# Attention, gated feed-forward and expert layer on one core: sweeps of 2, 3, 2 and 5 hidden units in place of 3, 2, 2 and 5, another order of weight conversions, one normalising product per head pair

## The chip, the core and the metric

The kernel runs on one core of one Trainium2 chip. The metric is the device time of one execution in microseconds (us). Before the change three runs gave 655.58, 655.60 and 659.03 us, median 655.6 us. One further execution was profiled; its own time was 655.69 us.

## What is computed

Three layers follow each other on 2 x 768 = 1536 tokens of 512 features.

```python
# 1. attention, 8 heads of 64: 8 global keys and the last 96 local ones, a slope per head
a = softmax(q @ k.T / 8 - slope * dist, kept keys only);  x = a @ v
# 2. gated layer, 512 -> 1536 -> 512
xn = x / sqrt(mean(x * x) + 1e-6) * rms_g
x = (silu(xn @ w_gate) * (xn @ w_val)) @ w_out
# 3. of 8 experts (512 -> 1024 -> 512) each token takes the one with the largest logit
out = p_max * (relu(x @ w1[e]) @ w2[e])
```

The weights of layer 2 (w_gate, w_val, w_out) come as 64-bit floats. Layers 2 and 3 multiply in a split form: each operand is a high part and the rest, and three products (high x high, high x rest, rest x high) make one.

## The kernel before, in words

Tokens are worked on in six stages of two tiles (256 tokens). The 1536 hidden features of layer 2 are 12 units of 128 (`m` = 0 to 11).

**Attention** (`fast_attention`, L410) takes 24 pairs of heads, four for each stage, and two tiles of each: 48 steps. A step computes scores on TensorE (L533 to L550), adds the distance table and takes the extremum on VectorE (L557), exponentiates on ScalarE (L561), transposes on TensorE (L572), copies the result on ScalarE (L580) and multiplies by the values (L601). After both tiles of a pair, `values` normalises: L608 and L609 make the reciprocals, and L611 multiplies, once for each tile. The first eight pairs use q and k as they are; from the ninth on they are split (L486 and L498 on ScalarE, L489 on GpSimd, L499 on VectorE). When the four pairs of a stage are done, `tail` (L381) normalises its rows and transposes them (L400, L403, L404); the stage is then "ready" for layer 2.

**Layer 2** (`moe_block`, L757) does a few units for one stage. A unit is 24 matmuls of 256 columns (L769: 12 with the gate weights, 12 with the value weights), then L777 to L787 on ScalarE, VectorE and GpSimd; after the units of a block, two tiles of output are accumulated, three matmuls of 512 columns for each unit and tile (L806). Sweep 0 writes the output sum to the tile (L813, ScalarE); later sweeps add to it (L815, VectorE). Sweep 0 goes over units 0 to 2 for all stages, the second sweep over 3 and 4, the third over 5 and 6, and the last over 7 to 11 (`M0`, `M1`, `range(lo, hi)`).

**Weight conversions** (`prep_steps`, L361): each unit needs three, gate, value and out. `load64` (L320) issues a 512 KB load on SyncE's queue into one of three `raw` buffers. `convert64` (L328) turns the 64-bit words into a high part and a rest: L334 on ScalarE, L337, L340, L343 and L346 on VectorE into one of two `cv` buffers, L353 on ScalarE, and L354 for the rest, on GpSimd during attention and on VectorE afterwards (`pin["sweep"]`). The results lie in a pool `wp` with three slots and a pool `ea` with four; `ea` shares its memory with attention's buffers and opens when attention has ended.

**Order.** The loop at L1165 writes the program: after each attention step it takes from `PREPS` which conversions are due (L1175), and for each step a credit of 0.5 (`MOE_RATE`) for matmuls of sweep 0 on stages that are ready. What is left of sweep 0 comes after attention (L1211) with one conversion of the next group (`PM[1]`) at each yield; the second and third sweep carry `PM[2]` and `PM[3]`, one conversion at every fourth or fifth yield (L1214). This is the order of priority; a scheduler with a model of time then sets the fixed order of each engine's instructions, and takes one that was written later where it finds an engine free and the operands and buffers there. A conversion written during attention is held behind the exponential of its step (L335); one of `PM[1]` has no such bond.

Of the kernel before, what the change touches and what calls it, by code (L numbers as in the profile page):

```python
# [14 lines left out]
ALU = mybir.AluOpType  # L15
# [4 lines left out]
P = 128  # L20
# [25 lines left out]
def kernel(  # L46
# [22 lines left out]
    FIRST = [0, 1, 1, 1, 1]  # L69
    M0 = [3] * NSTAGE  # L70
    M1 = 7
    PM = [[0, 1, 2], [3, 4, 5, 6], [7, 8, 9], [10, 11]]
    NHID = 6
# [3 lines left out]
    NRAW = 3  # L77
    PREPS = [2, 4, 6, 7, 11, 12, 20, 28, 36]
    NA = 3
# [210 lines left out]
    def body(is_fast):  # L290
# [69 lines left out]

        def prep_steps(ms, pool, nslot):  # L361

            steps = []
            for m in ms:
                def gv(i, w, m=m):
                    if i == 0:
                        weights[m, 0] = pool.tile([P, 2, 2, KD, P], F32R, tag="gv", bufs=nslot, name=f"gv{m}")
                    t = weights[m, 0]
                    raw = load64(w[:, m * P:(m + 1) * P].bitcast(U32).rearrange("(k p) f -> p k f", p=P), KD)
                    convert64(raw, t[:, i, 0].rearrange("p k f -> p (k f)"), t[:, i, 1].rearrange("p k f -> p (k f)"))  # L370

                def ow(m=m):
                    t = weights[m, 1] = pool.tile([P, 2, DM], F32R, tag="ow", bufs=nslot, name=f"ow{m}")
                    raw = load64(w_out[m * P:(m + 1) * P, :].bitcast(U32).rearrange("p (a f) -> p a f", a=1), 1)
                    convert64(raw, t[:, 0], t[:, 1])

                steps += [lambda gv=gv: gv(0, w_gate), lambda gv=gv: gv(1, w_val), ow]
            return steps

# [30 lines left out]
        def fast_attention(pool):  # L410
# [174 lines left out]
            def values(g, t, ptf, nb):  # L585
# [19 lines left out]
                if t == nt - 1:  # L605
                    rc = pool.tile([P, ST, 2], F32, tag="rc", bufs=2, name="rc")
                    xs3 = xp[:, 0:nt * VW].rearrange("p (t c) -> p t c", c=VW)
                    nc.vector.tensor_scalar(out=rc[:, 0:nt], in0=xs3[:, :, 0:VW:VW - 1], scalar1=1e-9, scalar2=None, op0=ALU.add)  # L608
                    nc.vector.reciprocal(rc[:, 0:nt], rc[:, 0:nt])  # L609
                    for tt in range(nt):  # L610
                        nc.vector.tensor_tensor(  # L611
                            out=part[STARTS[st] + tt][:, hp * P:(hp + 1) * P].rearrange("p (j d) -> p j d", j=2),
                            in0=xp[:, tt * VW + 1:tt * VW + 1 + P].rearrange("p (j d) -> p j d", j=2),
                            in1=rc[:, tt].unsqueeze(2).to_broadcast([P, 2, D]), op=ALU.mult,
                        )
                    groups[g] = None
# [537 lines left out]
        att = fast_attention(apool) if is_fast else dense_attention(apool)  # L1154
        preps = prep_steps(PM[0], wp, 3)
        ready = []
# [8 lines left out]
        while True:  # L1165
# [7 lines left out]
            if is_fast and nun == LATE:  # L1173
                late_loads()
            while preps and nun > PREPS[9 - len(preps)]:  # L1175
                preps.pop(0)()
            credit += MOE_RATE
            while True:
                if moe is None and ready:
                    st = ready.pop(0)  # L1180
                    moe = moe_block(0, range(M0[st]), st, mpool, False)
                    credit = 0.0
# [12 lines left out]
        ea = ea_cm.__enter__()  # L1195
        nx = prep_steps(PM[1], ea, 4)

# [13 lines left out]
        for st in ready:  # L1211
            run(moe_block(0, range(M0[st]), st, mpool, False))
        drain(f() for f in nx)
        for lo, hi, ms, pool, nslot, every in ((3, 5, PM[2], wp, 3, 4), (5, M1, PM[3], ea, 4, 5)):  # L1214
            nx = prep_steps(ms, pool, nslot)
            for st in range(NSTAGE):
# [163 lines left out]
```

## Time and profile before

| | before |
|---|---|
| median of three runs | 655.6 us |
| the profiled execution: its time / its span | 655.69 us / 654.0 us |
| granted TensorE clock, mean | 0.988 |
| TensorE matmul busy, weight load busy | 628.9 us (96%), 562.3 us (86%) |
| VectorE, ScalarE, GpSimd busy | 446.2, 320.3, 208.7 us (68%, 49%, 32%) |
| L769: 1728 matmuls; L806: 432 | 228.2 us; 113.9 us |

The span runs from the first to the last instruction of the profiled execution; 1.7 us of its time lie outside. Engines are PE (TensorE matmul), PEld (its weight load), DVE (VectorE), ACT (ScalarE), POOL (GpSimd) and SP (SyncE). Matmuls are pipelined, so busy times of neighbours overlap. Times in rows are counted from the start of the span.

### The profile page before, as it was taken

How to read it: one execution, taken by the hardware profiler on the slowest of the kernel's cores; microseconds unless marked ns; L12 is line 12 of the kernel's file. 1: busy time of each engine (PE TensorE's matmuls, PEld its weight loads, DVE VectorE, ACT ScalarE, POOL GpSimd, SP SyncE). 2: the span in 40 equal slices, each digit the busy share in tenths (PEclk: the TensorE clock that was granted, in tenths of full speed). 3: DMA queues.
4: the chain of work that ended last, by engine and by line, in shares of the span. 5: the costliest groups of instructions: out<-in, count | busy, mean ns of one | idle time of the engine just before them, and what ended most of it. 6: DMA issues, size and time to landing. Idle time of an engine off the chain costs nothing. (4 is left out here: it accounts for less than half of the span.)

```text
span 654.0 us, 11691 instructions
## 1 busy us (share of the span) xinstructions
PE 628.9 (96%) x4280; PEld 562.3 (86%) x4281; DVE 446.2 (68%) x1098; ACT 320.3 (49%) x624; POOL 208.7 (32%) x275
## 2 busy tenths in 40 slices
PE   9998998899999999999999999999999999999992
PEld 4667887899999999999999999997888899899891
DVE  5765888976599988676359998944667464664410
ACT  3666798777555533334622221333656564654420
POOL 4415758663122212111222532461610221011010
PEclk9999899899999999999999999999999999999997
DMA  7536466551044532131311010442978667454000
GB/s 228 158 90 201 127 174 181 157 149 39 1 130 130 161 98 72 59 98 65 129 65 65 2 65 34 122 138 82 301 261 261 206 217 253 168 189 140 17 13 30
DMA packets 56567, 82.98 MB, mean 127 GB/s; under 512 B 7983, under 2 KB 38703, under 8 KB 56496
## 3 DMA queue, kind: packets, MB, share of 16 engines
q1 hardware_dynamic: 53552, 74.75, 36.9%
q0 software_dynamic: 2944, 7.35, 3.4%
q8 instruction: 37, 0.61, 0.4%
q14 instruction: 34, 0.28, 0.1%
HBM read 75.75 MB, written 7.39 MB: 127 GB/s over the span
## 5 line engine op out<-in xcount | busy, mean ns | idle before, releaser
L769 PE MATMUL pg<-xn,gv 128*128 128x256 f32 x1728 | 228.2, 285 | 1.2 <-DVE th L778 1.2
L769 PEld LDWEIGHTS pg<-xn,gv 128*128 128x128 f32 x1728 | 220.2, 192 | 8.2 <-DVE th L778 1.5
L787 POOL TENSOR_TENSOR hid<-hf,hid 128x256 fp32r<-128x256 f32 x72 | 61.4, 855 | 174.6 <-ACT hid L786 174.5
L806 PE MATMUL po<-ow,hid 128*128 128x512 f32 x432 | 113.9, 394 | 0.0
L1017 PE MATMUL py<-ew,eh 128*128 128x512 f32 x384 | 91.2, 395 | 0.9 <-DVE eh L1084 0.5
L1017 PEld LDWEIGHTS py<-ew,eh 128*128 128x128 f32 x384 | 71.3, 188 | 17.7 <-DVE eh L1084 0.9
L806 PEld LDWEIGHTS po<-ow,hid 128*128 128x128 f32 x432 | 75.5, 189 | 11.7 <-POOL hid L787 0.3
L1039 PE MATMUL ph<-xs,ew 128*128 128x256 f32 x672 | 83.1, 283 | 0.0
L1039 PEld LDWEIGHTS ph<-xs,ew 128*128 128x128 f32 x672 | 81.6, 191 | 0.7
L786 ACT ACTIVATE hid<-hf 128x256 fp32r<-128x256 f32 x72 | 29.9, 417 | 83.7 <-DVE hf L782 81.9
L1024 POOL DMA_INDIRECT out_dram<-yo,tk x16 | 16.5, 1034 | 139.1 <-ACT yo L1023 107.7
L838 DVE CUSTOM_DVE_ANT_0 jk<-duo,rgb 128x512 bf16<-128x512 f32 x64 | 54.3, 849 | 0.5
L561 ACT ACTIVATE pr<-pr,mx 128x256 f32<-128x256 f32 (+1 forms) x96 | 45.1, 484 | 14.0 <-DVE mx L557 13.2
L957 DVE TENSOR_TENSOR ew<-rawe,ew 128x1024 fp32r<-128x1024 f32 (+1 forms) x36 | 40.8, 1134 | 12.9 <-ACT ew L953 12.9
L1048 DVE SCALAR_TENSOR_TENSOR eh<-ph,eh 128x256 fp32r<-128x256 f32 x56 | 23.1, 423 | 37.5 <-ACT eh L1047 35.5
L777 ACT ACTIVATE th<-pg 128x256 f32<-128x256 f32 x72 | 27.2, 379 | 39.8 <-PE pg L769 37.3
L957 DVE TENSOR_TENSOR ew<-duo,ew 128x1024 fp32r<-128x1024 f32 x28 | 34.1, 1224 | 17.9 <-ACT ew L953 16.8
L953 ACT ACTIVATE ew<-rawe 128x1024 fp32r<-128x1024 f32 x36 | 38.0, 1059 | 10.2 <-PE pg L769 4.6
L778 DVE SCALAR_TENSOR_TENSOR th<-th,pg 128x256 f32<-128x256 f32 x72 | 29.7, 415 | 16.4 <-ACT th L777 15.4
L1047 ACT ACTIVATE eh<-ph 128x256 fp32r<-128x256 f32 x56 | 21.2, 384 | 39.2 <-PE ph L1039 38.1
L953 ACT ACTIVATE ew<-duo 128x1024 fp32r<-128x1024 f32 x28 | 29.4, 1059 | 19.4 <-PE py L1017 19.4
L815 DVE TENSOR_TENSOR duo<-duo,po 128x512 f32<-128x512 f32 x36 | 23.4, 684 | 18.7 <-PE po L806 18.6
(178 smaller groups left out, 935.8 us busy)
## 6 DMA issues: line engine op xcount, KB each, us to landing
rawe<-in_moe_w_dram SPq DMA_DIRECT2D x36, 512.0 KB, 5.0
duo<-in_moe_w_dram SPq DMA_DIRECT2D x28, 512.0 KB, 5.4
raw<-in_moe_w_gate_dram SPq DMA_DIRECT2D x12, 512.0 KB, 3.8
raw<-in_moe_w_val_dram SPq DMA_DIRECT2D x12, 512.0 KB, 5.6
raw<-in_moe_w_out_dram SPq DMA_DIRECT2D x12, 512.0 KB, 3.4
kn<-in_k_dram SPq DMA_DIRECT2D x28, 192.0 KB, 3.3
qn<-in_q_dram SPq DMA_DIRECT2D x36, 128.0 KB, 2.9
vn<-in_v_dram SPq DMA_DIRECT2D x16, 192.0 KB, 2.6
```

Of the source, the lines that this page charges most:

```text
L561: pin["act"] = nc.scalar.activation(out=pr[:, j, 0:n], in_=pr[:, j, 0:n], func=ACTF.Exp, bias=mx[:, t, j:j + 1], scale=-1.0,)
L769: nc.tensor.matmul(out=pg[:, 0:n_], lhsT=gv[:, i, a, kk, :], rhs=x[st][:, kk, :], start=(n == 0), stop=(n == 3 * KD - 1),)
L777: pin["th"] = nc.scalar.activation(out=th, in_=pss[0][:, 0:n_], func=ACTF.Tanh, scale=0.5)
L778: nc.vector.scalar_tensor_tensor(out=th, in0=th, scalar=1.0, in1=pss[0][:, 0:n_], op0=ALU.add, op1=ALU.mult)
L786: nc.scalar.activation(out=hh[:, 0], in_=hf, func=ACTF.Copy)
L787: nc.gpsimd.tensor_tensor(out=hh[:, 1], in0=hf, in1=hh[:, 0].bitcast(F32), op=ALU.subtract)
L806: nc.tensor.matmul(out=po, lhsT=hid[mi][:, a, t * P:(t + 1) * P], rhs=ow[:, c, :], start=(mi == 0 and n == 0), stop=(mi == len(ms) - 1 and ...
L838: nc.vector.tensor_tensor_reduce(out=jk, in0=part[i0 + t], in1=rgb[e // 4][:, e % 4, :], scale=1.0, scalar=0.0, op0=ALU.mult, op1=ALU.add, ...
L953: cp = nc.scalar.activation(out=t[:, 0], in_=raw, func=ACTF.Copy)
L957: nc.vector.tensor_tensor(out=t[:, 1, 0:nd], in0=raw[:, 0:nd], in1=t[:, 0, 0:nd].bitcast(F32), op=ALU.subtract)
L1017: last_mm["py"] = nc.tensor.matmul(out=py, lhsT=hid(m, a, j), rhs=w2t[m // 2][:, c, (m % 2) * DM:(m % 2 + 1) * DM], start=(n == 0), stop=( ...
L1039: nc.tensor.matmul(out=ph[:, 0:CAP], lhsT=w1t[kk][:, a, m * P:(m + 1) * P], rhs=x[:, kk, :], start=(n == 0), stop=(n == 3 * KD - 1),)
```

## The change

Sweep 0 takes two units, the second sweep three (2, 3, 4). The groups of conversions are `[0, 1]`, `[2, 3, 4]`, `[5, 6, 7, 8]` and `[9, 10, 11]`, in place of `[0, 1, 2]`, `[3, 4, 5, 6]`, `[7, 8, 9]` and `[10, 11]`. During attention six conversions are due, after steps 2, 4, 6, 8, 11 and 18, and gate and value of both units come ahead of the two out weights. `slot` gives each unit the pool that it had. The third sweep takes a conversion at every fourth yield in place of every fifth. L611 becomes one product for both tiles of a pair.

```diff
--- before.py
+++ after.py
@@ -67,15 +67,15 @@
     XT = "ccccss"
     RING = "ccceewweec"
     FIRST = [0, 1, 1, 1, 1]
-    M0 = [3] * NSTAGE
+    M0 = 2
     M1 = 7
-    PM = [[0, 1, 2], [3, 4, 5, 6], [7, 8, 9], [10, 11]]
+    PM = [[0, 1], [2, 3, 4], [5, 6, 7, 8], [9, 10, 11]]
     NHID = 6
     MOE_RATE = 0.5
     NDV = 512
     HP = 0
     NRAW = 3
-    PREPS = [2, 4, 6, 7, 11, 12, 20, 28, 36]
+    PREPS = [2, 4, 6, 8, 11, 18]
     NA = 3
     MMA = "mm mm mm s s"
     MMB = "mm mm mm s s"
@@ -358,11 +358,15 @@
         weights = {}
         pin = {"act": None, "dve": None, "th": None, "sweep": False}
 
-        def prep_steps(ms, pool, nslot):
-
-            steps = []
+        def slot(m):
+            return (wp, 3) if m in (0, 1, 2, 7, 8, 9) else (ea, 4)
+
+        def prep_steps(ms, ow_last=False):
+
+            steps, ows = [], []
             for m in ms:
                 def gv(i, w, m=m):
+                    pool, nslot = slot(m)
                     if i == 0:
                         weights[m, 0] = pool.tile([P, 2, 2, KD, P], F32R, tag="gv", bufs=nslot, name=f"gv{m}")
                     t = weights[m, 0]
@@ -370,12 +374,14 @@
                     convert64(raw, t[:, i, 0].rearrange("p k f -> p (k f)"), t[:, i, 1].rearrange("p k f -> p (k f)"))
 
                 def ow(m=m):
+                    pool, nslot = slot(m)
                     t = weights[m, 1] = pool.tile([P, 2, DM], F32R, tag="ow", bufs=nslot, name=f"ow{m}")
                     raw = load64(w_out[m * P:(m + 1) * P, :].bitcast(U32).rearrange("p (a f) -> p a f", a=1), 1)
                     convert64(raw, t[:, 0], t[:, 1])
 
-                steps += [lambda gv=gv: gv(0, w_gate), lambda gv=gv: gv(1, w_val), ow]
-            return steps
+                steps += [lambda gv=gv: gv(0, w_gate), lambda gv=gv: gv(1, w_val)]
+                (ows if ow_last else steps).append(ow)
+            return steps + ows
 
 
         def tail(st, pool):
@@ -607,12 +613,11 @@
                     xs3 = xp[:, 0:nt * VW].rearrange("p (t c) -> p t c", c=VW)
                     nc.vector.tensor_scalar(out=rc[:, 0:nt], in0=xs3[:, :, 0:VW:VW - 1], scalar1=1e-9, scalar2=None, op0=ALU.add)
                     nc.vector.reciprocal(rc[:, 0:nt], rc[:, 0:nt])
-                    for tt in range(nt):
-                        nc.vector.tensor_tensor(
-                            out=part[STARTS[st] + tt][:, hp * P:(hp + 1) * P].rearrange("p (j d) -> p j d", j=2),
-                            in0=xp[:, tt * VW + 1:tt * VW + 1 + P].rearrange("p (j d) -> p j d", j=2),
-                            in1=rc[:, tt].unsqueeze(2).to_broadcast([P, 2, D]), op=ALU.mult,
-                        )
+                    nc.vector.tensor_tensor(
+                        out=duo[st][:, :, hp * P:(hp + 1) * P].rearrange("p t (j d) -> p t j d", j=2),
+                        in0=xs3[:, :, 1:P + 1].rearrange("p t (j d) -> p t j d", j=2),
+                        in1=rc[:, 0:nt].unsqueeze(3).to_broadcast([P, nt, 2, D]), op=ALU.mult,
+                    )
                     groups[g] = None
 
             warm(WARM1)
@@ -1152,7 +1157,8 @@
         apool_cm = tc.tile_pool(name="attn", bufs=1, side="right")
         apool = apool_cm.__enter__()
         att = fast_attention(apool) if is_fast else dense_attention(apool)
-        preps = prep_steps(PM[0], wp, 3)
+        preps = prep_steps(PM[0], True)
+        npreps = len(preps)
         ready = []
         moe = None
         credit = 0.0
@@ -1172,13 +1178,13 @@
             nun += 1
             if is_fast and nun == LATE:
                 late_loads()
-            while preps and nun > PREPS[9 - len(preps)]:
+            while preps and nun > PREPS[npreps - len(preps)]:
                 preps.pop(0)()
             credit += MOE_RATE
             while True:
                 if moe is None and ready:
                     st = ready.pop(0)
-                    moe = moe_block(0, range(M0[st]), st, mpool, False)
+                    moe = moe_block(0, range(M0), st, mpool, False)
                     credit = 0.0
                 if moe is None or credit <= 0:
                     break
@@ -1193,7 +1199,7 @@
         pin["act"], pin["sweep"] = None, True
         ea_cm = tc.tile_pool(name="ea", bufs=1, side="right")
         ea = ea_cm.__enter__()
-        nx = prep_steps(PM[1], ea, 4)
+        nx = prep_steps(PM[1])
 
         yields = [0]
 
@@ -1209,10 +1215,10 @@
         if moe is not None:
             run(moe)
         for st in ready:
-            run(moe_block(0, range(M0[st]), st, mpool, False))
+            run(moe_block(0, range(M0), st, mpool, False))
         drain(f() for f in nx)
-        for lo, hi, ms, pool, nslot, every in ((3, 5, PM[2], wp, 3, 4), (5, M1, PM[3], ea, 4, 5)):
-            nx = prep_steps(ms, pool, nslot)
+        for lo, hi, ms, every in ((M0, 5, PM[2], 4), (5, M1, PM[3], 4)):
+            nx = prep_steps(ms)
             for st in range(NSTAGE):
                 run(moe_block(1, range(lo, hi), st, mpool, False), every)
             drain(f() for f in nx)
```

## Rows read from the trace of the kernel before

**Rows 1.** Windows: us, then PE, PEld, DVE, ACT, POOL busy, granted clock, DMA share, GB/s

```profile
50.00:65.00 15.00, 12.77 (x100) 10.63 (x99) 7.25 (x30) 9.09 (x18) 8.42 (x10) 1.00 0.67 192
65.00:82.00 17.00, 15.78 (x117) 14.78 (x117) 15.30 (x38) 13.72 (x30) 12.57 (x21) 0.90 0.47 127
82.00:98.00 16.00, 15.03 (x123) 13.97 (x123) 13.98 (x55) 14.81 (x36) 8.73 (x13) 1.00 0.61 175
98.00:115.00 17.00, 14.99 (x113) 13.72 (x112) 14.68 (x46) 14.14 (x32) 13.85 (x20) 1.00 0.68 175
115.00:131.00 16.00, 13.80 (x99) 13.09 (x98) 15.05 (x35) 11.91 (x26) 11.13 (x14) 0.89 0.58 161
131.00:147.00 16.00, 16.00 (x133) 15.61 (x132) 11.50 (x44) 11.81 (x26) 10.66 (x19) 1.00 0.55 153
```

**Rows 2.** Waits of TensorE, 0 to 180 us: us in total, times, longest

```profile
PE sp L550 <- DVE mx L557: 4.6, 7, 1.4
PE pp L572 <- ACT ptS L580: 2.2, 1, 2.2
PE pg L769 <- DVE th L778: 1.2, 1, 1.2
```

**Rows 3.** Windows of L769 alone: us, PE and PEld busy (x instructions), clock, DMA

```profile
82.00:98.00 16.00, 2.13 (x12) 1.62 (x12) 1.00 0.61 175
98.00:115.00 17.00, 3.77 (x24) 3.11 (x24) 1.00 0.68 175
```

**Rows 4.** Timeline of TensorE, first block's output: start, us, engine, line

```profile
102.17 2.89 PE L806 MATMUL po<-ow,hid 128*128 128x512 f32 x12
...
126.06 1.08 PE L806 MATMUL po<-ow,hid 128*128 128x512 f32 x4
```

**Rows 5.** Timeline of ScalarE: conversions begin (L334), stages become ready (L403)

```profile
64.27 0.58 ACT L403 ACTIVATE xn<-trx 128x512 fp32r<-128x512 f32 x1
...
77.49 0.66 ACT L334 ACTIVATE cv<-raw 128x512 f32<-128x512 f32 x1
...
92.20 0.59 ACT L403 ACTIVATE xn<-trx 128x512 fp32r<-128x512 f32 x1
...
112.03 0.65 ACT L334 ACTIVATE cv<-raw 128x512 f32<-128x512 f32 x1
113.06 0.66 ACT L334 ACTIVATE cv<-raw 128x512 f32<-128x512 f32 x1
```

**Rows 6.** Windows of the conversions' tile cv: DVE, ACT, POOL busy (x instructions)

```profile
115.00:131.00 16.00, 9.26 (x11) 1.29 (x2) 1.27 (x1) 0.89 0.58 161
131.00:174.00 43.00, 0.00 (x0) 0.00 (x0) 0.00 (x0) 1.00 0.26 72
```

**Rows 7.** Timeline of VectorE, a conversion instruction of attention

```profile
117.52 1.82 DVE L340 TENSOR_SCALAR cv<-cv 128x512 uint32<-128x512 uint32 x1
```

**Rows 8.** Groups by line: busy us, mean ns | idle before

```profile
L340 DVE TENSOR_SCALAR cv<-cv 128x512 uint32<-128x512 uint32 x36 | 17.5, 485 | 0.3
...
L611 DVE TENSOR_TENSOR duo<-xp,rc 128x128 f32<-128x128 f32 x48 | 12.0, 285 | 0.5
L782 DVE SCALAR_TENSOR_TENSOR hf<-th,pg 128x256 f32<-128x256 f32 x72 | 29.8, 415 | 7.1 <-PE pg L769 5.5 <-issue 0.6
```

**Rows 9.** Timeline of ScalarE, the first wait for a split pair's keys

```profile
62.24 0.84 ACT L486 ACTIVATE kt<-kn 128x768 fp32r<-128x768 f32 x1 [2.43 <-DMA kn<-in_k_dram]
```

**Rows 10.** Timelines after attention: outputs (L813, L815) and conversions' ends (L354)

```profile
176.42 0.59 ACT L813 ACTIVATE duo<-po 128x512 f32<-128x512 f32 x1
...
191.93 0.68 DVE L354 TENSOR_TENSOR gv<-cv,gv 128x512 fp32r<-128x512 f32 x1
192.89 0.69 DVE L354 TENSOR_TENSOR ow<-cv,ow 128x512 fp32r<-128x512 f32 x1
...
283.18 1.28 DVE L815 TENSOR_TENSOR duo<-duo,po 128x512 f32<-128x512 f32 x2
...
307.26 1.29 DVE L815 TENSOR_TENSOR duo<-duo,po 128x512 f32<-128x512 f32 x2 [1.16 <-PE po L806]
```

## The prediction, made before the changed kernel was run

> **What bounds it now.** I read the windows of the whole core first, then TensorE's waits, then the timelines around them. From 131 to 147 us, with layer 2 beside attention, TensorE is busy all of the time at full clock [rows 1], and over the whole span it is busy 96%. From 82 to 131 us, in attention, it is not: it idles 0.97, 2.01 and 2.20 us in three stretches (16 less 15.03, and so on), 5.2 us in all, and the granted clock of the last is 0.89 (a mean of the levels 2.4 and 1.2 GHz, after such gaps), which costs 0.11 x 16 = 1.8 us [rows 1]. From 50 to 82 us it idles another 2.23 and 1.22 us, with 0.10 x 17 = 1.7 us of clock [rows 1]. The waits behind this are short ones: scores waiting for the extremum on VectorE, 4.6 us in 7 waits; one of 2.2 us for ScalarE; one of 1.2 us for a VectorE product of layer 2 [rows 2]. So TensorE bounds the kernel, and a reordering can win only what it idles in attention.
>
> The second thing to see is what TensorE has to fill such gaps with. Between 82 and 115 us only 12 + 24 = 36 matmuls of layer 2's units ran [rows 3], though the first stage had been ready since 65 us (its second tile was turned at 64.27 us) [rows 5]. Its third unit was held by its weights: their conversions began at 77.49 and 112.03 us (first and last of three) [rows 5]. The 12 output matmuls of units 0 and 1 stand at 102.17 us, the last four of unit 2 only at 126.06 us [rows 4]. The second stage, turned at 92.20 us, had to queue behind that block [rows 5].
>
> **The change part by part.**
>
> *Two units in sweep 0.* Matmuls are neither added nor removed: 12 units, four outputs per tile. What moves is when they can run. Price: in the third sweep a two-unit block took (307.26 - 283.18) / 3 = 8.0 us [rows 10], that is 48 matmuls of 256 columns and 12 of 512; by columns 0.111 and 0.222 us each. Before, 82 to 115 us held 36 x 0.111 + 12 x 0.222 = 6.7 us of this. After, the first block needs no third unit, so it holds 12 outputs of the first stage (2.7 us) and all of the second stage's block (8.0 us, from about 93 us): 10.7 us, 4.0 more. The gaps from 82 to 131 us offer 5.2 + 1.8 = 7.0 us, so 4.0 fit. The work is then missing between 131 us and the end of attention, but TensorE was full there, so attention itself passes sooner. The bounds are 0 (gaps that are waits in a fixed order stay although there is work) and 7.0 us (all of it). I take 4.0: the full stretch after 131 us, with filler at hand, shows no idle at all [rows 1], and that is the nearest row.
>
> *Conversions.* During attention six are due in place of nine, but nothing holds the others back: before, the first conversion of the next group began at 113.06 us, 1.03 us after the last due one, although it was written behind attention [rows 5]. Unit 2 goes to a pool that is open, so its three conversions will follow the one due after step 18 (near 70 us) as fast as the three raw and two cv buffers allow (step 20 was at 77.49 us, so 70 is an estimate), and two of unit 3 will stand in cv until attention ends, as two did before. Eleven are done or begun in attention both times. In 115 to 131 us eleven VectorE instructions on cv took 9.26 us [rows 6], four to a conversion, so 3.4 us each; from 131 to 174 us none ran [rows 6]. Three or four such lots move from 98 to 131 us into 65 to 98 us. I take 0 for that: VectorE was busy 29.3 of 33 us in the one and 29.7 in the other [rows 1]. Below nothing it can go by the waits for VectorE, 4.6 + 1.2 = 5.8 us in all of attention [rows 2], above by the 9.9 us that the slower rival prices; between these the equal load is the nearest row.
>
> *Loads.* Their number stays at 36. On SyncE's queue, which they share with the loads of q, k and v, the value load of unit 2 moves ahead and its out load back (its raw buffer comes free only with the conversion after step 18), both away from the keys of the first split pairs. ScalarE waited 2.43 us for such keys at 62.24 us [rows 9], and TensorE's 2.2 us wait and the clock dip behind it follow from that. A load with no buffer blocks what is queued behind it, so the cost is bounded by -3.9 (wait and dip both go) and +2.2 us (a second such wait). The keys' own buffers come free only when an earlier pair's scores are done, so I take 0.
>
> *One product per pair.* Two instructions of 285 ns overlap (12.0 us busy for 24 pairs, 0.50 a pair); one of twice the size should take what L782, also 256 columns out of PSUM, takes: 0.415 us [rows 8]. 24 x 0.085 = 2.0 us of VectorE. On the path lie at most the pairs between 50 and 131 us, half of them: 0 to 1.0 us. I take 0, since 4.0 already counts the gaps.
>
> *Hand-over to the second sweep.* At 176.42 us three blocks of three units were out [rows 10]: nine units, 4.5 blocks of two. The other 1.5 blocks take 12.0 us, to 188.4; then units 2 and 3 of the first stage 48 x 0.111 = 5.3 us, to 193.7. Unit 4's value weights, the next to be late, are wanted 1.3 us on, at 195.1, and were ready at 191.93 + 0.68 = 192.6 [rows 10]. That is 2.5 us in hand. If TensorE arrives 4.0 us sooner and attention's memory does not, 1.5 us are lost. I take 0.
>
> *Later conversions.* Twelve in the second sweep (six blocks of 12.0 us: 6.0 us for each) and nine in the third (5.3 us each) in place of nine and six. They lie beside a full TensorE: the third sweep kept its 8.0 us pace [rows 10] and carried six. Without that cover a late one would cost up to its 3.4 us.
>
> **Sum.** 655.7 (the profiled execution, 0.1 us above the median of the runs) - 4.0 = 651.7 us.
>
> **Rivals.**
>
> *Nothing moves.* The same eleven conversions run in attention and the gaps are waits for VectorE in a fixed order, which filler cannot enter. For it: the longest waits name L557, not missing work [rows 2]. Against: no wait shows from 131 us on, with the same scores and plenty of filler. Time: 655.7 less up to 1.0 us of products, 655.
>
> *Slower: VectorE is choked between 66 and 100 us.* The late out conversion, three of unit 2 and two of unit 3 crowd there; four more than before at 3.4 us are 13.6 us from 65 to 98 us, where 3.7 us are free [rows 1, 6], and scores wait 9.9 us longer for L557. Filler of 4.0 us covers part: 5.9 us lost, 661.5 us. It decides once a conversion stands ahead of scores for longer than the filler of one stage lasts. For it: with GpSimd busy 11.1 of 16 us [rows 1] an L340 took 1.82 us [rows 7], and its mean is 0.485 [rows 8]. Against: a conversion that is not due ranks behind scores. The Trainium skill ("SBUF — State Buffer", Who interferes with whom) says that some VectorE instructions (tensor_scalar in its two-port modes, those with two SBUF inputs against a reading GpSimd) and GpSimd's exclude each other for a whole instruction; the slow L340 agrees, and by that rule early conversions would also hold up GpSimd's split of the keys, and the time would be this rival's.
>
> *More than filled.* All idle and clock loss from 50 to 131 us goes: 8.6 + 3.5 = 12.1 us, 643.6 us. For it: both dips follow gaps of one to two us. Against: the wait for keys is untouched.
>
> **How the numbers follow.** Forecast 0.45, nothing 0.28, slower 0.17, more 0.10. About 0.5% (3.3 us) is what a measurement of this kernel tells from no change: 652.3 and 658.9 us. The forecast's own range is 649 to 653.5, of which I put 0.35 under 652.3 and 0.10 above. So faster 0.35 + 0.10 = 0.45, same 0.10 + 0.28 = 0.38, slower 0.17. The range leaves out half of the outer two cases: 647 to 660 us.
>
> **What would show it.** Right: the first stage's twelve output matmuls done before 90 us, in place of 127, more than 48 L769 matmuls between 82 and 115 us, idle of 82 to 131 us near 1 to 2 us with clock 1.00, and the stretch behind attention still full. L611 24 times at 0.42 us. Wrong: conversions of unit 2 with score waits at 66 to 100 us as long as those at 78 to 120 us now; idle in front of unit 4's matmuls; or an attention that ends as late as before with TensorE idle at 131 to 171 us, for lack of filler.

## The result and the profile after

The change makes the kernel slower: 663.59 us (median of four runs, 662.64 to 664.90) against 655.59 us (four runs) on the same chip, a ratio of 1.0102 with an interval of 1.0072 to 1.0132. The forecast was 651.7 us, and 660 us was the top of the range. The profiled execution took 664.19 us, with a span of 662.5 us (before 654.0) at a mean clock of 0.976 (before 0.988). In all experiments below, ratios leave out single runs more than 1.5% above the fastest of their kernel (one each of e1 and e12, one of the kernel before beside e16 and e17), while medians hold all runs.

The windows of the whole core, for the stretches of [rows 1] and the two behind them. Columns: stretch, its length, busy us and count of PE, PEld, DVE, ACT and POOL, then clock, DMA share and GB/s.

```profile
50.00:65.00 15.00, 12.67 (x87) 10.70 (x86) 8.20 (x28) 10.20 (x20) 7.77 (x11) 0.86 0.57 157
65.00:82.00 17.00, 15.05 (x96) 12.92 (x95) 16.80 (x35) 11.30 (x25) 11.78 (x16) 0.90 0.51 152
82.00:98.00 16.00, 12.86 (x78) 11.71 (x78) 13.86 (x39) 12.65 (x27) 5.31 (x10) 0.81 0.50 152
98.00:115.00 17.00, 15.89 (x108) 15.42 (x108) 11.95 (x36) 11.52 (x28) 7.42 (x10) 0.80 0.63 174
115.00:131.00 16.00, 15.12 (x118) 14.15 (x118) 13.95 (x45) 13.36 (x29) 10.65 (x17) 1.00 0.44 124
131.00:147.00 16.00, 14.65 (x122) 13.76 (x122) 12.62 (x42) 13.69 (x30) 11.25 (x21) 1.00 0.61 168
147.00:164.00 17.00, 15.52 (x131) 14.83 (x131) 11.33 (x42) 12.59 (x30) 10.44 (x18) 1.00 0.22 60
164.00:180.00 16.00, 16.00 (x124) 15.16 (x123) 7.30 (x17) 7.69 (x19) 2.90 (x4) 1.00 0.00 2
```

The last two stretches of the kernel before, which [rows 1] does not hold:

```profile
147.00:164.00 17.00, 17.00 (x139) 16.38 (x138) 10.53 (x38) 12.17 (x26) 6.99 (x14) 1.00 0.13 37
164.00:180.00 16.00, 16.00 (x126) 15.32 (x125) 9.19 (x25) 9.13 (x21) 2.76 (x6) 1.00 0.00 1
```

TensorE now idles 3.14 us from 82 to 98 us (before 0.97) and 1.35 us from 131 to 147 us, where it had idled nothing [rows 1]. The clock fell to 0.81 and 0.80 from 82 to 115 us, where it had been 1.00. Idle time and lost clock ((1 - clock) x length) from 50 to 180 us are 12.24 + 10.24 = 22.5 us, against 8.6 + 3.5 = 12.1 us: 10.4 us more, while the span grew by 8.5 us. From 180 to 440 us TensorE idles in neither kernel, and the clock is 1.00. The loss is in attention.

What TensorE lacked there is seen in the unit matmuls alone (the line that was L769 is L774 now), same stretches, columns PE and PEld:

```profile
65.00:82.00 17.00, 7.24 (x43) 6.44 (x42) 0.90 0.51 152
82.00:98.00 16.00, 0.00 (x0) 0.00 (x0) 0.81 0.50 152
98.00:115.00 17.00, 7.99 (x45) 7.37 (x46) 0.80 0.63 174
115.00:131.00 16.00, 3.06 (x24) 2.79 (x24) 1.00 0.44 124
131.00:147.00 16.00, 1.04 (x7) 0.66 (x6) 1.00 0.61 168
147.00:164.00 17.00, 4.44 (x31) 3.87 (x31) 1.00 0.22 60
```

From 82 to 98 us, where TensorE idles longest and its clock has fallen, not one unit matmul ran, and from 131 to 147 us seven, in place of 48 in the kernel before:

```profile
131.00:147.00 16.00, 7.13 (x48) 6.17 (x47) 1.00 0.55 153
```

The totals up to 180 us are these: the first two rows are of the kernel after, the last two of the kernel before (line, matmul, count, busy, mean ns).

```profile
L774 PE MATMUL pg<-xn,gv 128*128 128x256 f32 x213 | 33.5, 310 | 0.4 <-DVE mx L563 0.4
L811 PE MATMUL po<-ow,hid 128*128 128x512 f32 x45 | 14.0, 420 | 0.1
```

```profile
L769 PE MATMUL pg<-xn,gv 128*128 128x256 f32 x261 | 41.6, 302 | 1.2 <-DVE th L778 1.2
L806 PE MATMUL po<-ow,hid 128*128 128x512 f32 x54 | 14.4, 398 | 0.0
```

At the prices of the prediction (0.111 and 0.222 us, from [rows 10]) that is 33.63 us of layer 2 done by 180 us in place of 40.96. The missing 7.3 us come behind attention, where TensorE is full, and there they cost their whole length.

The conversions are the second thing that moved. All instructions on tile cv from 65 to 98 us (columns DVE, ACT, POOL), before and then after:

```profile
65.00:98.00 33.00, 5.68 (x8) 1.96 (x3) 1.29 (x1) 0.95 0.54 151
```

```profile
65.00:98.00 33.00, 18.38 (x23) 5.08 (x8) 1.28 (x1) 0.85 0.50 152
```

Nothing holds the conversions of later units back any more, and they stand where the prediction put them: the five that are not due (three of unit 2, two of unit 3) begin at 63.58 (with the last out weights), 73.05, 78.92, 89.22 and 94.17 us on ScalarE. VectorE carries 12.7 us more there. The waits of TensorE up to 180 us that are longest (total us, times, longest):

```profile
PE sp L556 <- DVE mx L563: 3.6, 5, 0.9
PE pp L578 <- ACT ptS L586: 2.1, 2, 1.9
PE xp L607 <- DVE duo L616: 1.9, 3, 1.0
PE sp L556 <- POOL kt L427: 1.4, 2, 1.1
```

Scores wait less for VectorE than in [rows 2]; the wait for the product L616 is new, and the wait for ScalarE's copy behind the keys is still there. So no single wait carries the loss; many gaps do (from 82 to 115 us all waits are under 1 us), with too little layer 2 to put into them: from 82 to 98 us two output matmuls ran, and nothing else of it.

### The profile page after: what moved, and what is told of

It is laid out like the page before. It is cut to its first block, busy times and chain, and to the rows that moved or that the text cites. A ratio compares the mean times of both kernels' runs of the same rounds, so it can differ in the third digit from the quotient of the medians.

```text
span 662.5 us, 11661 instructions
## 1 busy us (share of the span) xinstructions
PE 634.1 (96%) x4280; PEld 566.4 (85%) x4281; DVE 446.9 (67%) x1077; ACT 318.7 (48%) x624; POOL 203.2 (31%) x272
## 5 line engine op out<-in xcount | busy, mean ns | idle before, releaser
L774 PE MATMUL pg<-xn,gv 128*128 128x256 f32 x1728 | 225.1, 285 | 0.4 <-DVE mx L563 0.4
L774 PEld LDWEIGHTS pg<-xn,gv 128*128 128x128 f32 x1728 | 219.4, 193 | 6.7 <-DVE mx L563 0.6
L567 ACT ACTIVATE pr<-pr,mx 128x256 f32<-128x256 f32 (+1 forms) x96 | 44.0, 482 | 13.9 <-DVE mx L563 13.6
```

Of the source, the lines that this page charges most:

```text
L567: pin["act"] = nc.scalar.activation(out=pr[:, j, 0:n], in_=pr[:, j, 0:n], func=ACTF.Exp, bias=mx[:, t, j:j + 1], scale=-1.0,)
L774: nc.tensor.matmul(out=pg[:, 0:n_], lhsT=gv[:, i, a, kk, :], rhs=x[st][:, kk, :], start=(n == 0), stop=(n == 3 * KD - 1),)
```

## The experiments

Each ratio is to the kernel before on the same chip, with a 95% interval. A conversion without a bond to a step of attention is called free here. Two explanations stood against each other at first: layer-2 work is short in attention (**filler**), or VectorE's early conversions hold attention up (**conversions**).

**e1: the two-unit kernel, without conversions in attention that are not due.** Those of units 2 to 4 are bound behind attention's last exponential.

```diff
+        last_exp = pin["act"]
         pin["act"], pin["sweep"] = None, True
...
-            pin["act"] = pin["th"] if every > 1 else None
+            pin["act"] = pin["th"] if every > 1 else last_exp
```

> The changed kernel, but the nine conversions of units 2, 3 and 4 are bound behind the last exponential of attention, so that none of them can enter attention. Theory (early conversions choke VectorE from 64 to 98 us, and TensorE idles and loses clock there): idle and clock loss between 50 and 115 us fall from 8.5 + 10.2 us to the 2 + 2 us of the wait for the first split keys, attention ends 5 to 10 us earlier; what is then missing comes behind attention, where unit 2 is converted late, 0 to 8 us; time 652 to 660 us. Rival (two units in the first sweep leave too little filler): attention stays as in the changed kernel, and the late conversions add to it; 663 to 670 us.

Measured: 657.82 us, 0.9995 (0.9966 to 1.0024): by the ratio the whole loss is gone, with two units kept. The next conversion begins at 151.56 us, and tile cv takes VectorE 4.23 us from 65 to 98 us. Yet the unit matmuls come as unevenly as in the kernel after (PE and PEld columns):

```profile
82.00:98.00 16.00, 1.12 (x4) 1.00 (x5) 0.79 0.44 126
98.00:115.00 17.00, 8.15 (x45) 7.13 (x45) 0.90 0.37 110
115.00:131.00 16.00, 3.50 (x24) 3.05 (x24) 1.00 0.59 161
131.00:147.00 16.00, 0.00 (x0) 0.00 (x0) 1.00 0.44 120
```

The nine of its ten runs that count spread from 653.81 to 661.89 us, and the profiled one (661.89 us, span 660.2 us) was the slowest of them, so its rows do not show a run of median time: idle time and lost clock from 50 to 115 us are 5.5 + 6.9 us in it, not the 2 + 2 us that the expectation named. What follows: the conversions that are not due are part of the cost, while the holes at 82 to 98 and 131 to 147 us belong to two units and stay.

**e2: unit 2 converted in attention as before, after steps 24, 30 and 36.**

```diff
-    PREPS = [2, 4, 6, 8, 11, 18]
+    PREPS = [2, 4, 6, 8, 11, 18, 24, 30, 36]
...
-        preps = prep_steps(PM[0], True)
+        preps = prep_steps(PM[0], True) + prep_steps([2])
...
-        nx = prep_steps(PM[1])
+        nx = prep_steps(PM[1][1:])
```

> The changed kernel, but the three conversions of unit 2 are due in attention after steps 24, 30 and 36, bound to the exponentials of those steps and with the rest taken on GpSimd, as before the change. Two units stay in the first sweep. Theory (crowding): the stretch 64 to 98 us loses its extra idle and clock loss, 654 to 657 us. Rival (two units leave too little filler, whatever the conversions do): 661 to 664 us.

Measured: 667.83 us, 1.0162 (1.0132 to 1.0191). Spreading the conversions over attention does not help: it made +0.6% here and, with two products for a pair, -0.3% (e4 against e10, below).

**e3 and e4: the product alone.** e3 is the kernel before with the change's one product for a pair and nothing else of it, e4 the kernel after with the two products of before. The diff is e3's, shortened; e4's is the reverse.

```diff
-                    for tt in range(nt):
-                        nc.vector.tensor_tensor(
-                            out=part[STARTS[st] + tt][:, hp * P:(hp + 1) * P].rearrange("p (j d) -> p j d", j=2),
...
+                    nc.vector.tensor_tensor(
+                        out=duo[st][:, :, hp * P:(hp + 1) * P].rearrange("p t (j d) -> p t j d", j=2),
...
```

> The kernel before with the one product per pair alone. Theory (the product is worth at most 1 us on the path): 654.5 to 656 us. Rival (one product ends later than the first of two, and the values matmuls wait for it; three such waits of 1.9 us stand in the changed kernel): 657 to 660 us.

> The changed kernel with the two products of before. Theory: 663 to 665 us, the product is no part of the loss. Rival (waits of the values matmuls for the product): 659 to 661 us.

Measured: e3 661.83 us, 1.0058 (1.0041 to 1.0075); e4 671.45 us, 1.0214 (1.0183 to 1.0245). The product costs the one kernel 0.6% and saves the other 1.1%. An instruction of 0.4 us for 24 pairs cannot do both by its length; each edit also makes the scheduler set the order of all queues anew.

**e5 and e6: fill the gaps with useless matmuls** in steps 18 to 33, e5 on e1 and e6 on the kernel after.

```diff
-                if un < WARMU:
+                if un < WARMU or 18 <= un < 34:
```

> The kernel of the run with bound conversions, and two idle-filling matmuls (no result is used) after the scores of each of the steps 18 to 33, as the first sixteen steps have them. Theory (with two units there is no filler between the end of the first block near 82 us and the second stage near 92 us; TensorE then falls below 2.4 GHz, 5 us between 82 and 115 us in that kernel): the granted clock of 82 to 115 us rises from 0.79 and 0.90 to above 0.95 and the time falls by 2 to 5 us against the run with the bond alone. Rival (the clock is low because TensorE waits, and the waits set the time): same idle, the 32 extra matmuls of 0.22 us add up to 7 us.

> The changed kernel with the same idle-filling matmuls in steps 18 to 33. Theory (clock loss of 10.2 us from 50 to 115 us is a loss of its own): 657 to 661 us with the clock of 82 to 115 us above 0.95. Rival (it only mirrors the waits on VectorE): 663 to 669 us.

Measured: e5 666.54 us, 1.0167 (1.0122 to 1.0212); e6 675.02 us, 1.0310 (1.0263 to 1.0357). In e5 the clock from 82 to 115 us was 1.00 in place of e1's 0.79 and 0.90, and the kernel was 1.7% slower than e1: layer 2 done by 180 us fell from 241 and 54 matmuls to 213 and 42. But the clock was lost elsewhere: 0.75 from 65 to 82 us and 0.91 and 0.87 from 115 to 147 us, where e1 has 0.93, 1.00 and 1.00. Over 50 to 180 us the lost clock is 8.7 us in e5 and 6.9 in e1, and 10.3 in e6 against 10.2 in the kernel after. So the useless matmuls moved the dips and took room from layer 2; what a lasting full clock would be worth is not shown. e6 and e5 differ in the bond of e1 alone, which is worth 1.4% here, as it was worth 1.1% between the kernel after and e1.

**e7 and e8: the conversions alone, with three units.** e7 is the kernel before with unit 2's conversions written after step 18 without a bond; e8 is the kernel before with e1's bond for units 3 to 6.

```diff
-    PREPS = [2, 4, 6, 7, 11, 12, 20, 28, 36]
+    PREPS = [2, 4, 6, 7, 11, 12, 18, 18, 18]
...
             while preps and nun > PREPS[9 - len(preps)]:
+                held = pin["act"], pin["sweep"]
+                if len(preps) <= 3:
+                    pin["act"], pin["sweep"] = None, True
                 preps.pop(0)()
+                pin["act"], pin["sweep"] = held
```

> The kernel before, three units in the first sweep, but the conversions of unit 2 written after step 18, without the bond to an exponential and with the rest on VectorE, as the changed kernel has them early. Theory of crowding (early conversions choke VectorE whatever the units): 660 to 664 us. Rival (the loss is filler: with three units the early conversions even let unit 2 run sooner): 653 to 657 us.

> The kernel before with its twelve conversions of units 3 to 6 bound behind the last exponential of attention, so that the two of unit 3 that entered at 113 and 125 us stay out. Theory (conversions that nothing in attention needs cost waits and clock there): the idle and clock loss of 115 to 131 us (2.2 + 1.8 us) fall below 1.5 us, time 1 to 4 us under the kernel before. Rival (the hand-over needs them early): 656 to 662 us.

Measured: e7 657.68 us, 1.0019 (1.0001 to 1.0037); e8 656.41 us, 0.9983 (0.9953 to 1.0013). In e7 the five free conversions ran from 52.85 to 73.17 us, and there, earlier than in the kernel after, they cost 0.2%, hardly to be told from no change. The bond of e1, which was worth 1.1% with two units, is worth no more than 0.2% here (e8).

**e9 and e10: e7 and e2 with the other product.** e9 is e7 with one product, e10 is e2 with two; the diffs are those of e3 and e4.

> The kernel before with early conversions of unit 2 and with one product: against the changed kernel only the units of the first sweep differ (three, not two; gate, value and out weights also keep their old order). Theory (two units leave attention short of useful matmuls; the early conversions alone are harmless): 655 to 660 us, 0.5 to 1 per cent under the changed kernel. Rival (the product or the crowding makes the loss): 662 us or more.

> Two units in the first sweep, unit 2 converted late and bound in attention after steps 24, 30 and 36, two products: against the kernel before only the units of the first sweep and the order of the first six conversions differ. Theory (short of useful matmuls): 663 to 670 us, with no matmuls of layer 2 between 82 and 98 us. Rival: 655 to 659 us.

Measured: e9 654.59 us, 0.9968 (0.9945 to 0.9991), the lowest ratio of all; e10 669.67 us, 1.0183 (1.0140 to 1.0227).

**e11: spread the holes out.** e1, with each half unit bound behind the scores of its step and a larger credit.

```diff
-    MOE_RATE = 0.5
+    MOE_RATE = 1.2
...
+                            if n == 0 and pin["mm"] is not None:
+                                behind(first, pin["mm"])
```

> The kernel with bound conversions and two units, with each half unit of the first sweep held behind the scores of the attention step that it is written after, and a credit of 1.2 for a step, so that a block of 8.0 us is spread over the eight steps of a stage and does not run as one lump. Theory (the gaps come from the lump: nothing is left between two blocks): L774 matmuls in all stretches from 65 to 147 us, clock of 82 to 115 us above 0.95, 650 to 656 us. Rival (the amount is short, however it is spread): idle moves but does not fall, 656 to 664 us.

Measured: 668.55 us, 1.0183 (1.0145 to 1.0222). From 131 to 147 us one unit matmul ran, and by 180 us 240 and 54 of layer 2's matmuls were done, no more than in e1: for that stretch the work was used up, not badly spread. That expectation failed, and the rival's 656 to 664 us too. It loses more behind attention too: from 180 to 230 us TensorE idles 4.1 us at a clock of 0.97, in e1 1.1 us at 1.00.

**e12 and e15: e7 with e1's bond**, with two products (e12) and with one (e15); the diffs are those of e1, e7 and e3.

> The kernel before with unit 2 converted early and the conversions of units 3 to 6 bound behind attention: three units of matmuls for attention as soon as a stage is ready, and no conversion there that attention does not need. Theory: 651 to 656 us, under the kernel before by 0.1 to 0.7 per cent. Rival (hand-over waits take it back): 657 to 661 us.

> The kernel before with unit 2 converted early, one product, and the conversions of units 3 to 6 bound behind attention. Theory: the best of all, 650 to 655 us, under the kernel before by 0.3 to 0.9 per cent. Rival (late conversions take back at the hand-over what attention gains): 655 to 658 us.

Measured: e12 655.14 us, 0.9981 (0.9956 to 1.0006); e15 661.08 us, 1.0050 (1.0027 to 1.0074). e15 should have been the best kernel and was not. Against e12 it differs in the product (+0.7%), against e9 in the bond (+0.8%), and no run tells which of the two to blame. With three units the bond thus made -0.2 (before, e8), -0.4 (e7, e12) and +0.8% (e9, e15).

**e13: one unit in sweep 0**, to double the suspected cost.

```diff
-    M0 = 2
+    M0 = 1
...
-    PM = [[0, 1], [2, 3, 4], [5, 6, 7, 8], [9, 10, 11]]
+    PM = [[0], [1, 2, 3, 4], [5, 6, 7], [8, 9, 10, 11]]
...
-    PREPS = [2, 4, 6, 8, 11, 18]
+    PREPS = [2, 4, 11]
...
-        for lo, hi, ms, every in ((M0, 5, PM[2], 4), (5, M1, PM[3], 4)):
+        for lo, hi, ms, every in ((M0, 5, PM[2], 4), (5, M1, PM[3], 3)):
```

> The changed kernel with one unit in the first sweep and four in the second. Theory (useful matmuls for attention: a stage gives 4.0 us in place of 8.0): another 1 to 2 per cent, 668 to 677 us, with less layer-2 work done by 180 us than in the changed kernel (213 matmuls of units). Rival (the loss is not the units): 658 to 665 us.

Measured: 677.98 us, 1.0296 (1.0238 to 1.0353), just above the filler theory's 668 to 677 us. Eleven conversions begin in attention, as in the kernel after, so their number is not what differs.

**e14, e16, e17 and e18: units, order and due step apart.** e14 is the kernel after with three units in sweep 0 (unit 2's conversions written behind step 18, without a bond, by the same lines as in e7; the second sweep then takes a conversion at every third yield in place of every fourth). e18 is e14 with the sixth conversion due after step 12 in place of 18, e17 is the kernel after with that, and e16 is the kernel after with the order and the first six steps of before.

```diff
-    M0 = 2
+    M0 = 3
...
-    PM = [[0, 1], [2, 3, 4], [5, 6, 7, 8], [9, 10, 11]]
+    PM = [[0, 1], [3, 4], [5, 6, 7, 8], [9, 10, 11]]
...
-    PREPS = [2, 4, 6, 8, 11, 18]
+    PREPS = [2, 4, 6, 8, 11, 18, 18, 18, 18]
...
-        preps = prep_steps(PM[0], True)
+        preps = prep_steps(PM[0], True) + prep_steps([2])
```

This is e14's, without those two parts; in e18 `PREPS` is `[2, 4, 6, 8, 11, 12, 18, 18, 18]`. The next is e16's; in e17 `PREPS` alone is changed, to `[2, 4, 6, 8, 11, 12]`.

```diff
-    PREPS = [2, 4, 6, 8, 11, 18]
+    PREPS = [2, 4, 6, 7, 11, 12]
...
-        preps = prep_steps(PM[0], True)
+        preps = prep_steps(PM[0])
```

> The changed kernel with three units in the first sweep and two in the second; unit 2 is written after step 18 in attention, without the bond and with the rest on VectorE, everything else as changed (gate and value first, out weights after steps 11 and 18, one product). Theory (units): 653 to 658 us, 260 or more matmuls of units done by 180 us. Rival (the new order of the first conversions): 661 to 667 us.

> The changed kernel with the old order and steps of the first six conversions (2, 4, 6, 7, 11, 12). Theory (the out weights due after step 18 hold five unbound conversions behind them into 64 to 98 us, where VectorE has no room): the five run between 50 and 76 us, and the time is 654 to 658 us. Rival (two units): 661 to 666 us.

> The changed kernel with the last due conversion after step 12 in place of 18, gate and value weights still first. Theory: as with the old order, 654 to 658 us. Rival (gate and value first, or two units): 661 to 666 us.

> Edit: e14 with the last output weights of the first sweep due after step 12 instead of step 18; three units, gate and value weights first, unit 2's conversions free as in e14. Theory A (the late due step makes e14's loss, since the conversions behind it fall between 64 and 91 us, where VectorE is short): conversions before 75 us as in e9, ratio 0.995 to 1.002, about 655 us, waits of scores for VectorE back under 3 us. Theory B (converting gate and value weights first, so that the output weights come last, costs by itself): 1.006 to 1.013, about 662 us, even with conversions before 75 us. Theory C (neither; a reordering of this size moves the time by half a per cent to one per cent either way): between the two, with idle and clock loss in other stretches than in e14.

Measured: e14 663.50 us, 1.0100 (1.0049 to 1.0152); e16 665.13 us, 1.0121 (1.0098 to 1.0144); e17 665.62 us, 1.0119 (1.0089 to 1.0149); e18 658.49 us, 1.0023 (0.9998 to 1.0048).

e9 and e16 have the same product, and their free conversions begin at the same times (50.30 to 75.02 and 50.78 to 75.21 us); they differ in the units, 0.9968 against 1.0121. e18 and e17 are such a pair with the new order, 1.0023 against 1.0119. So two units in place of three cost 1.0 to 1.5% with the conversions early. The unit matmuls of e9, then of e16 (PE, PEld):

```profile
65.00:82.00 17.00, 11.16 (x70) 9.82 (x69) 0.83 0.68 190
82.00:98.00 16.00, 0.00 (x0) 0.00 (x0) 1.00 0.42 124
98.00:115.00 17.00, 11.14 (x72) 9.47 (x72) 1.00 0.56 165
115.00:131.00 16.00, 6.38 (x41) 5.35 (x41) 1.00 0.40 111
```

```profile
65.00:82.00 17.00, 7.89 (x48) 6.70 (x46) 0.83 0.72 198
82.00:98.00 16.00, 0.00 (x0) 0.00 (x0) 0.89 0.52 151
98.00:115.00 17.00, 7.66 (x48) 6.51 (x48) 0.90 0.47 134
115.00:131.00 16.00, 3.52 (x24) 3.06 (x24) 1.00 0.52 139
```

Each stage hands e9 a block of 72 unit matmuls and e16 one of 48 at the same pace of attention (the second stage was ready at 97.0 and 96.4 us). From 82 to 98 us e9 still has the block's 18 output matmuls (5.10 us) and full clock; e16 has five (1.33 us), and 0.89.

e18 and e14 differ in the due step, with three units. The whole core from 50 to 98 us, e18 and then e14 (columns as in the first fence):

```profile
50.00:65.00 15.00, 11.14 (x68) 8.90 (x67) 13.50 (x36) 10.61 (x20) 8.23 (x11) 0.85 0.76 209
65.00:82.00 17.00, 17.00 (x130) 16.62 (x130) 16.76 (x37) 11.69 (x27) 11.47 (x13) 0.93 0.66 182
82.00:98.00 16.00, 13.39 (x105) 12.13 (x104) 10.19 (x40) 13.16 (x30) 8.65 (x17) 1.00 0.48 135
```

```profile
50.00:65.00 15.00, 12.49 (x93) 10.54 (x92) 7.90 (x28) 9.59 (x19) 6.88 (x11) 0.93 0.57 155
65.00:82.00 17.00, 14.30 (x103) 12.62 (x102) 16.96 (x35) 11.98 (x27) 10.48 (x14) 0.96 0.54 141
82.00:98.00 16.00, 13.77 (x96) 12.09 (x95) 16.00 (x44) 11.64 (x25) 7.43 (x11) 1.00 0.60 188
```

With step 12 the conversions use VectorE's room before 65 us (13.50 of 15 us busy in place of 7.90); with step 18 VectorE is busy 32.96 of 33 us from 65 to 98 us, 19.83 of them on tile cv (8.81 in e18), and scores wait for it 4.5 us in 9 waits in place of 2.4 in 4. That costs three units 0.8%, as e18's Theory A had it, though its ratio lies just above that theory's 0.995 to 1.002. With two units the step does not matter (1.0102 and 1.0119).

**All profiles together.** Layer-2 work done by 180 us (unit matmuls x 0.111 us + output matmuls x 0.222 us, counted in each trace) beside the span:

| kernel | units | unit / output matmuls by 180 us | work, us | span, us | ratio |
|---|---|---|---|---|---|
| e18 | 3 | 283 / 54 | 43.4 | 652.2 | 1.0023 |
| e12 | 3 | 282 / 54 | 43.3 | 651.3 | 0.9981 |
| e7 | 3 | 279 / 54 | 43.0 | 652.5 | 1.0019 |
| e9 | 3 | 272 / 54 | 42.2 | 652.3 | 0.9968 |
| e8 | 3 | 269 / 54 | 41.8 | 656.4 | 0.9983 |
| before | 3 | 261 / 54 | 41.0 | 654.0 | 1 |
| e3 | 3 | 245 / 54 | 39.2 | 657.7 | 1.0058 |
| e1 | 2 | 241 / 54 | 38.7 | 660.2 | 0.9995 |
| e14 | 3 | 232 / 54 | 37.7 | 659.8 | 1.0100 |
| e16 | 2 | 235 / 48 | 36.7 | 659.7 | 1.0121 |
| e15 | 3 | 228 / 49 | 36.2 | 659.4 | 1.0050 |
| after | 2 | 213 / 45 | 33.6 | 662.5 | 1.0102 |
| e2 | 2 | 208 / 42 | 32.4 | 664.7 | 1.0162 |
| e17 | 2 | 203 / 42 | 31.9 | 665.6 | 1.0119 |
| e4 | 2 | 199 / 40 | 31.0 | 668.1 | 1.0214 |
| e10 | 2 | 167 / 36 | 26.5 | 669.7 | 1.0183 |
| e13 | 1 | 144 / 34 | 23.5 | 676.0 | 1.0296 |

Each span is that of the one profiled execution (in e7, e14 and e16 the fastest of its kernel, in e1 and e8 the slowest that counts), so it does not always go with the ratio. Each us of layer 2 that attention does not take lengthens the span by 1.15 us (a straight line through these 17 rows; correlation -0.98). A slope near 1 follows from counting alone, since the amount of work is fixed and TensorE, in the kernels before and after, idles nowhere from 180 to 440 us: the line shows where the time goes, and not why. Left out are e5, e6 and e11, whose edits put other matmuls or bonds into attention; e5 and e6 lie within 2 us of the line, e11 7.8 us above it (38.6 us of work, span 665.6 us).

The two losses leave different marks. From 82 to 115 us every kernel of the table with two units or one has a stretch at a clock of 0.75 to 0.89; of the nine with three, eight have 1.00 in both stretches and e3 has 0.90 in one. The kernels e14 and after have the same ratio, but from 50 to 180 us e14 loses 13.4 us to idling and 3.5 to the clock, and after 12.2 and 10.2.

## Why the prediction was wrong

**What bounds it** was read rightly: TensorE, and what a reordering can change is its idle time in attention. The loss is there and nowhere else.

**Step "Two units in sweep 0"** failed, and with it the sign. It said that 82 to 115 us would hold 10.7 us of layer 2 in place of 6.7. It held 45 x 0.111 + 2 x 0.222 = 5.4 us: the first block's outputs were done before 82 us, as hoped (10 of 12), but the second stage was ready only at 98.5 us, so nothing was left until then. The step counted what could start sooner inside one chosen stretch, and not the supply. A stage that becomes ready gives attention 8.0 us of layer 2 with two units and 12.0 us with three, and taking it sooner only empties the store sooner. The sentence that the stretch behind 131 us may starve without cost, "since attention itself passes sooner", was the error itself: starved, TensorE waits for attention's own chain (1.35 us idle in that stretch in place of none, as shown above), and attention did not pass sooner. Its last tile was turned by 181.98 us, 2.6 us later than before (the kernel before, with its last two tiles in one row, then after):

```profile
178.30 1.09 ACT L403 ACTIVATE xn<-trx 128x512 fp32r<-128x512 f32 x2
...
181.38 0.60 ACT L409 ACTIVATE xn<-trx 128x512 fp32r<-128x512 f32 x1
```

Even where attention does pass sooner it does not pay: in e13, with one unit, that tile was turned by 172.03 us, and the kernel was 1.9% slower than after.

**Step "Conversions"** had the place right, near 64 to 98 us, and took the wrong price. The move was given as 13.6 us at 3.4 each; VectorE got 12.7 us more on cv. It was priced at 0 because VectorE was equally busy in the stretches before and after the move; but only 3.7 us were free in the one. It also missed that unit 2's conversions, without the bond, have their rest (L354) on VectorE and not on GpSimd: one took 1.90 us at 76.99 us. With three units the crowding costs 0.8% (e14 against e18). The slower rival, which put 661.5 us on this, came nearest, but was only half of the matter: with two units the same loss stands when the conversions are early (e16, e17).

The two causes do not add up. Two units with early conversions 1.2%, three units with late ones 1.0%, both 1.0%. And two units with only the six that are due cost nothing that the ratio shows (e1). So the hole of the step above was costly only together with conversions that were not due. A reading that fits these four, argued and not shown: with three units TensorE's work sets attention's pace and hides up to eleven conversions, if they are not crowded; with two it does not, and VectorE's conversions then count wherever they lie. e11 and e15 do not follow from it.

**VectorE beside GpSimd.** VectorE's L340 took 827 ns on average from 65 to 98 us after (five of them), against 466 before (two). In the kernel after, one that ran while GpSimd idled took 0.41 us, and one beside GpSimd's split of the keys 1.50 us. It ended 0.28 us behind that split, and so did the slow one of [rows 7] (the last line is GpSimd in the kernel before):

```profile
83.53 0.41 DVE L340 TENSOR_SCALAR cv<-cv 128x512 uint32<-128x512 uint32 x1
...
93.38 1.50 DVE L340 TENSOR_SCALAR cv<-cv 128x512 uint32<-128x512 uint32 x1
...
93.09 1.51 POOL L495 TENSOR_TENSOR kt<-kn,kt 64x512 fp32r<-64x512 f32 x1 [2.13 <-issue]
...
117.25 1.81 POOL L489 TENSOR_TENSOR kt<-kn,kt 64x768 fp32r<-64x768 f32 x1 [0.44 <-POOL kt L421]
```

That is in accord with the Trainium skill ("SBUF — State Buffer", Who interferes with whom), which has certain VectorE instructions and GpSimd's shut each other out; no run here separates it from other causes. The splits of 64x512 took 1.46 to 1.62 us from 82 to 98 us, before 1.27 to 1.52, so the hold-up of the keys that the slower rival feared is about 0.2 us for each split.

**Loads**: 0 was taken, with -3.9 as the best case; the wait for the copy behind the keys is still there (1.9 us), so 0 stands. **One product**: the size was right, 24 at 421 ns:

```profile
L616 DVE TENSOR_TENSOR duo<-xp,rc 128x256 f32<-128x256 f32 x24 | 10.1, 421 | 0.6
```

Its effect was not the 0 to 1.0 us gain of the bounds. In five pairs that differ in it alone it made +0.6 (before, e3), -0.5 (e7, e9), +0.7 (e12, e15), -0.2 (e10, e2) and -1.1% (e4, after). The bounds counted the instruction and left out that the fixed order of all queues is worked out anew. So a single difference of up to 1% between two kernels here is not evidence about the edit, the change's own 1.0% included. What counts is what came back in more than one pair: the bond with two units (-1.1 and -1.4%), the third unit with early conversions (-1.5 and -1.0%), and the lower clock from 82 to 115 us with two units. The 0.8% of e14 against e18 stands on one pair, and e9's 0.3% gain belongs to that kernel and not to a rule. **Hand-over** and **later conversions**: right, no idle from 180 to 440 us.

**Rivals.** That nothing moves was wrong, since much moved; "more than filled" had the wrong sign. The case that happened stood only under what would show the forecast wrong, "TensorE idle at 131 to 171 us, for lack of filler", and had no price and no chance. Its price could have been had from [rows 10]: 12.0 - 8.0 = 4.0 us less for each stage, and four stages are ready by 145 us (after: 61, 98, 126 and 145 us), 16 us less to fill attention with, against a gain of 4.0 us. Measured by 180 us it was 7.3 us less, since the kernel before did not use up its own four stages either (41.0 of 48.0 us).

## What to carry to other kernels

Where independent work fills a stage that waits on a chain, count the whole supply of that work against the whole stage, and not only how soon its first piece can start; what is not done there costs its full length where the engine is full. Before making work optional in a stage, look whether anything keeps the scheduler from pulling it in anyway: six due conversions became eleven, and with two units one bond was worth 1.1 and 1.4% (with three it gave nothing that can be relied on). And test an edit in more than one surrounding, where a fixed order is worked out anew for every edit.

## What was not expected of the hardware

The clock fell where TensorE was still busy 80% of the time (from 82 to 98 us 12.86 of 16 us, clock 0.81), with no wait in the list over 1 us: but for two output matmuls the work there was attention's own, and between the levels of 1.2 and 2.4 GHz the stretch lay at 0.81 on average. Useless matmuls kept the clock at 1.00 where they stood (e5, 82 to 115 us), but over 50 to 180 us e5 lost more clock than e1 (8.7 against 6.9 us). Why the runs of e1 that count spread over 8 us, and those of e9 over 2 us, stays open.
